# Three passes for the second expert of the first 448-column chunk, weights split in another order, and one row load moved, in a fused attention and expert kernel

## The chip, the cores and the metric

The kernel runs on one core of a Trainium2 chip. The metric is the device time of one execution in microseconds. The profile shows one execution; its times count from the start of the span.

## The reference

The first half is attention with a sketched kernel: q and k (4 batches, 4 heads, 1088 tokens, 32 wide) are each multiplied by two small matrices S1 and S2 (8 x 32), and the outer product of the two results is a feature of 64 numbers. The second half puts the heads side by side (4352 tokens, 128 wide) and runs four experts on every token, weighted by normalized probabilities.

```python
q_p, k_p = phi(q), phi(k)               # outer products of S1 x and S2 x, 64 features
kv = np.einsum('bhsf,bhsd->bhfd', k_p, v)
z = np.sum(k_p, axis=2)
x = (q_p @ kv) / (q_p @ z + 1e-6)       # per head; then heads side by side: (4352, 128)
p = domain_probs / (domain_probs.sum(-1, keepdims=True) + 1e-09)
for e in range(4):                      # w1[e]: 128 x 1024, w2[e]: 1024 x 128
    h = np.maximum(x @ w1[e], 0.0)
    out += p[:, e:e + 1] * (h @ w2[e])
```

All data is float32.

## The kernel before, in words

**Chunks and steps.** The tokens are the columns of all expert products. They are cut into chunks of 128, 448, 512, seven times 448, and 128 columns (`CHUNKS`, counted m = 0, 1, 2 and on). For each chunk the four experts follow each other, and for each expert the 1024 hidden rows are taken as eight blocks of 128, two blocks (a pair) to a step. So a chunk has `NQ` = 16 steps; step i is chunk i // 16, expert (i % 16) // 4, pair i % 4. A step has two half steps, j = 0 and 1, one block each. A half step is written (i.j) here: (20.0) is the first half of chunk 1's second expert (expert 1), (24.0) the first half of its third.

**Two kinds of product.** A plain product multiplies float32 operands directly. A product in three passes splits each operand into a high and a low part of a narrower type (`fp32r` in the profile) and a third, mixed part, and adds three products: for the first layer `xa`·`wa` (L1105), `xb`·`wb` (L1106) and `xd`·`wd` (L1154). Between the second and the third pass ScalarE scales the sum in PSUM in place (L1107, `h<-h`). The third pass of a half step is issued by `third()`, which is called in the next half step, after that one's first two passes. Then ScalarE makes the hidden tile: for blocks whose second product is in three passes (`THREE`, six of eight) the high part `ha` (L1157), from which VectorE makes `hb` (L1131) and, for two blocks at once, `hd` (L1134); for the others a plain relu, `hid` (L1162). The second layer's products are issued some half steps later by a list of due times (`to_due`, `DEAL`, `behind`; L1203 where the expert is plain, L1222 otherwise). VectorE adds their two sums into `ev` (L1254) after ScalarE copied one (L1225 or, for plain experts, L1251), and GpSimd multiplies by the gate and adds to the total (L1261, L1263).

**Which product is of which kind before.** Chunk 0 and the last chunk are plain throughout. In chunk 1 the first two experts are plain (`whole`: L1092 for the first layer with `hid` at L1094, L1203 for the second). All else is in three passes.

**Split weights.** `weight_parts(e)` makes `wa` on ScalarE and `wb`, `wd` on VectorE, 512 columns at a time, over four steps. `second_weight_parts(e)` makes `vab` on ScalarE twice (768 columns) and `vab`, `vb`, `vd` on VectorE, over two steps. `token_parts(m)` makes `xa` on ScalarE and `xb`, `xd` on VectorE for a chunk. All go through `split` (L882) and `join` (L885). The table `to_part` says after which step each is called; what is called at the end of a step stands on each engine's queue behind that step's own work.

**Attention beside the experts.** The tokens of chunk m must exist before the chunk starts. Attention is cut into units (`UNITS`); unit 1 of batch 0 is chunk 0, unit 2 (448 rows) chunk 1, and unit 3 (512 rows) chunk 2. Unit 2's stages on VectorE run during chunk 0; they end in a transposition `y` (L694) and copies into the tile `ring` on ScalarE and GpSimd (L706). Unit 3 is transposed (`qturn`), projected on TensorE (L243, `qT,sx`), copied by ScalarE (`qs`, L755), stored to DRAM (`qd`) and read back broadcast (`qp`, `qb`), multiplied on VectorE (L776), multiplied with the keys' sums on TensorE (`kvx`), divided, transposed to `y`, stored (`xd`) and loaded into `ring`. Batch 1's keys follow: transposition (`kT`, L383), projection (L426, `sk,kT`), `fs` and `vx` copies on ScalarE (L429, L392, L397), products on VectorE (L442). These pieces stand in one list, `plan`, each with a cost and, for some, a number of half steps that must lie between it and an earlier piece. `work()`, called once in every half step, adds a credit by the room that is left until the next chunk (`rate`, `rooms`, `EARLY`) and runs pieces while the credit lasts.

**Queues.** Nearly all DMAs are issued by SP, in program order. The rows of q for units 2 and 3 of batch 0 are one load (`load_rows(q, 0, "qn", slice(P, S))`, 960 columns) ahead of all expert weights; then follow `w1` of expert 0 (L141), the probabilities, `w2` of expert 0 (L154), and `w1`, `w2` of experts 1 to 3.

Of the kernel before, what the change touches and what calls it, by code (L numbers as in the profile page):

```python
# [24 lines left out]
def kernel(  # L25
# [26 lines left out]
    P = 128  # L52
# [45 lines left out]
    def load_rows(src, b, name, part=slice(0, S)):  # L98

        d = kn if name == "kn" else qn  # L100
        if b not in d:
            d[b] = lpool.tile([P, S], F32, tag=name, name=name)
        c, n = part.start, part.stop - part.start
        base = src.offset + b * H * S * D
        if name == "qn" and b == B - 1:
            for c, n, t in ((0, (G - 4) * D, 0), ((G - 4) * D, 4 * D, S - P)):
                nc.sync.dma_start(d[b][:, c : c + n], bass.AP(src.tensor, base + t * D, [[S * D, H], [n, 32], [1, n]]))
        else:
            nc.sync.dma_start(d[b][:, part], bass.AP(src.tensor, base + c, [[G * D, P], [1, n]]))
# [70 lines left out]

    ends = cpool.tile([P, 2, E], F32, name="ends")
    e_sum = cpool.tile([P, 2, 3], F32, name="e_sum")
    load_rows(q, 0, "qn", slice(P, S))
    load_w1(0)
    for p0, n, g0, m, t in ((0, 96, 0, G, 0), (96, 32, 0, G - 4, 3 * S), (96, 32, G - 4, 4, B * S - P)):
        nc.sync.dma_start(
# [9 lines left out]
    for e in range(1, E):  # L196
        load_w1(e)
        load_w2(e, 0)
        load_w2(e, 1)
    sk = cpool.tile([P, P], F32, name="sk")  # L200
    sp = apool.tile([32, 3, 2, 32], F32, tag="qf", name="sp")
    sr = cpool.tile([P, 3, 2, P], F32, tag="sr", name="sr")
# [592 lines left out]
    def add(cost, run, name, after=None):  # L795

        plan.append((cost, run, name, after))

    def lay_plan():

        of_first = queries(0, P, UNITS[0][1])
        costs = [0.62] * 9 + [0.05] * 4 + [0.4, 0.55, 0.6, 0.1, 0.1]
        for at, cost in enumerate(costs):
            add(cost, lambda: next(of_first, None), f"first{at}", ("first8", 5) if at == 12 else ("first12", 2) if at == 13 else None)
        covers.append((len(plan), P + UNITS[0][1]))
        add(vector_us(later[0][2]), lambda: unit_turn(0), "qturn")
        add(0.1, lambda: unit_project(0), "visit", ("qturn", 7))
        add(0, lambda: None, "wait", ("start", 2 * NQ + 2))
        keys = {}
        for b in range(1, B):  # L810
            now_on, plan[:] = list(plan), []
            key_pieces(b)
            keys[b], plan[:] = list(plan), now_on
        for w, (b, c, n, u) in enumerate(later):
            if b == 0:
                plan.extend(keys[1][:3])
            else:
                at = {(1, 0): (1, 3, 13), (1, 1): (2, 0, 3), (1, 2): (2, 3, 5), (2, 0): (2, 5, 13)}
                at.update({(2, 1): (3, 0, 3), (2, 2): (3, 3, 9), (3, 0): (3, 9, 13)})
                if (b, u) in at:  # L820
                    k, z0, z1 = at[b, u]
                    plan.extend(keys[k][z0:z1])
                if u == 0:
                    key_end(b)
            more = w + 1 < len(later)
            if more:
                add(vector_us(later[w + 1][2]), lambda w=w: unit_turn(w + 1), "qturn")
            for p in range(2):
                add(vector_us(n), lambda w=w, p=p: unit_product(w, p), "product", ("visit", LAND if w else LAND + 3))

            def visit(w=w, more=more):
                if more:
                    unit_project(w + 1)
                unit_visit(w)

            add(0.1, visit, "visit", ("product", 3 if w < 4 else 2))
            add(0.4, lambda w=w: inverse.__setitem__(w, attend_inverse(*products[w])), "inverse", ("visit", 1))
            add(vector_us(n), lambda w=w: over.__setitem__(w, attend_scale(*products[w], inverse.pop(w))), "scale")
            add(vector_us(n), lambda w=w: unit_out(w), "out")
            covers.append((len(plan), S * b + c + n))  # L840
# [196 lines left out]
    def whole(m, e):  # L1037
        return m == 1 and e < E // 2

    begun_hp, made_hp = {}, {}  # L1040

    def half_columns(i, hp, c):
# [11 lines left out]
    def first(i, work, between=None):  # L1054

        m, kq = steps[i]
        n, (e, f) = CHUNKS[m], divmod(kq, NP)
        if plain(m):
            third()
            lower()  # L1060
            hd = hidden()
            hid[i] = [hd[:, n * j : n * j + n] for j in range(2)]
            if i in begun_hp:
                hp = begun_hp.pop(i)
                half_columns(i, hp, HP)
            elif i in made_hp:
                hp = made_hp.pop(i)
            else:
                hp = psum(ps_h, "h")
                for j in range(2):  # L1070
                    both(
                        hp[:, n * j : n * j + n],
                        w1_of[e][:, P * (2 * f + j) : P * (2 * f + j + 1)],
                        (x_last if m else x_first)[:, :],
                        start=True,
                        stop=True,
                    )
            if m and kq % 2:
                nc.vector.tensor_scalar(
                    out=hd[:, 0 : 2 * n], in0=hp[:, 0 : 2 * n], scalar1=0.0, scalar2=None, op0=ALU.max  # L1080
                )
            else:
                nc.scalar.activation(hd[:, 0 : 2 * n], hp[:, 0 : 2 * n], ACTF.Relu)
            work()
            work()
            return
        hid[i] = []
        if whole(m, e):
            ((x, _, _),) = placed(START[m], n)
            for j in range(2):  # L1090
                hp = psum(ps_h, "h")[:, 0:n]
                nc.tensor.matmul(hp, w1_of[e][:, P * (2 * f + j) : P * (2 * f + j + 1)], x, start=True, stop=True)  # L1092
                u = hidden()[:, 0:n]
                nc.scalar.activation(u, hp, ACTF.Relu)  # L1094
                hid[i].append(u)
                work()
                if j == 0:
                    between(0)
            return
        xa, xb, xd_ = (x[:, 0:n] for x in xparts[m])  # L1100
        for j in range(2):
            k = 2 * f + j
            g = psum(ps_h, "h")[:, 0:n]
            w = slice(P * k, P * (k + 1))
            nc.tensor.matmul(g, wa[:, e, w], xa, start=True, stop=False)  # L1105
            nc.tensor.matmul(g, wb[:, e, w], xb, start=False, stop=True)  # L1106
            nc.scalar.activation(g, g, ACTF.Copy, scale=1.0 + R12)  # L1107
            third()
            hid[i].append(None)
            begun.append((i, j, k, g, wd[:, e, w], xd_))  # L1110

            if any(d[0] <= 2 * i + j and d[5] and d[5] + str(2 * (steps[d[3]][1] % NP) + d[4]) == last_of[1] for d in due):
                between(j)
                lower()
                work()
            else:
                lower()
                work()
                if j == 0:
                    between(0)  # L1120
# [28 lines left out]
    def third():  # L1149

        while begun:
            i, j, k, g, w, x = begun.pop(0)
            n = g.shape[-1]
            nc.tensor.matmul(g, w, x, start=False, stop=True, skip_group_check=True)  # L1154
            if in_three(k):
                (ha, hb, hc), both_of = three_tiles(k, n)
                nc.scalar.activation(ha, g, ACTF.Relu, scale=NEAR)  # L1157
                to_lower.append((g, ha.bitcast(F32), hb, both_of))
                hid[i][j] = ha, hb, hc
            else:  # L1160
                hid[i][j] = hidden()[:, 0:n]
                nc.scalar.activation(hid[i][j], g, ACTF.Relu)  # L1162
# [152 lines left out]
        begun_hp[i] = psum(ps_h, "h")  # L1315
        half_columns(i, begun_hp[i], 0)
    to_part = {}
    for e, at, then in zip((2, 3, 0, 1), (8, 15, 15, 18), (18, 20, 26, 32)):
        for at, parts_of in ((at, weight_parts(e)), (then, second_weight_parts(e))):
            for step in range(at, at + 4):  # L1320
                to_part.setdefault(step, []).append(parts_of)
    for m in range(1, NC - 1):
        at, tokens = NQ * m - 4 if m > 1 else NQ + 4, token_parts(m)
        for step in (at, at + 1):
            to_part.setdefault(step, []).append(tokens)
    ending = iter(())
# [42 lines left out]
    for i in range(len(steps) + LA):  # L1369
        if i < len(steps):  # L1370
# [2 lines left out]
            rate = max(  # L1373
                [0]
                + [
                    (needed[c] - spent[0]) / max(sum(rooms[2 * i : 2 * NQ * c - (EARLY if c > 1 else 2)]), 0.3)
                    for c in range(m + 1, NC)
                    if 2 * NQ * c - (EARLY if c > 1 else 2) > 2 * i
                ]
            )  # L1380

# [68 lines left out]
```

## Time and profile before

| what | value |
|---|---|
| times of the kernel before | 456.1, 456.46 and 496.8 us, median 456.46 |
| the profiled execution's own time | 456.12 us |
| its span | 454.3 us |
| granted TensorE clock in the span | 1.00 |
| busy: TensorE, VectorE, ScalarE, GpSimd | 447.6, 359.7, 329.3, 119.0 us |
| HBM read, written | 32.68 MB, 5.21 MB |
| chunk 0's experts on TensorE | about 13.4 to 30.1 us |
| chunk 1, experts 0 and 1 | about 30.1 to 56.4 us |
| chunk 1, experts 2 and 3 | about 56.4 to 79.4 us |

Rows of the profile name an engine, a source line, an operation, the tile written and the tiles read. PE is TensorE's products, PEld its weight loads, DVE VectorE, ACT ScalarE, POOL GpSimd, SPq the issuing of DMAs by SP. A plain float32 product is recorded as two rows (x2). The recorded length of a row is not the distance to the next one: rows of an engine overlap in the record, so the pace is read from the starts. A bracket at the end of a row is idle time of the engine just before it and what ended it. The chain of waits is the work that ended last, followed back from the end.

### The profile page before, as it was taken

What the parts mean: (1) busy time and instruction counts of PE and PEld (TensorE: products, weight loads), DVE (VectorE), ACT (ScalarE), POOL (GpSimd) and SP (SyncE); (2) the same over time, 40 slices, a digit from 0 to 9 for tenths busy, and PEclk for the clock granted to TensorE, in tenths of its full rate; (3) what the DMA queues carried; (4) which work ended last, traced back from release to release, by engine and by line L of the source; (5) the groups of instructions that cost most, each with busy time, mean ns of one, the idle gap of its engine ahead of it and who ended that gap; (6) DMA issues with size and microseconds to landing.
All of it is one profiled execution on the core that took longest, in us unless ns stands there. A gap on an engine that the chain in (4) does not pass through costs nothing.

```text
span 454.3 us, 8639 instructions
## 1 busy us (share of the span) xinstructions
PE 447.6 (99%) x3005; PEld 366.1 (81%) x3005; DVE 359.7 (79%) x600; ACT 329.3 (72%) x695; POOL 119.0 (26%) x206
## 2 busy tenths in 40 slices
PE   9999999999999999999999999999999999999997
PEld 6765587777778888888988888888888888888886
DVE  6867669988888797889877998787779787887753
ACT  4366588866877695788786867787778788877731
POOL 6462122410232123212221232124223212322320
PEclk9999999999999999999999999999999999999999
DMA  7884252024313353052423511320320121027401
GB/s 213 281 189 119 67 169 78 24 45 109 119 51 75 82 111 57 20 138 72 122 64 47 143 25 28 94 75 21 87 57 24 37 45 41 21 41 218 147 2 27
DMA packets 53716, 38.45 MB, mean 85 GB/s; under 512 B 27113, under 2 KB 49961, under 8 KB 53673
## 3 DMA queue, kind: packets, MB, share of 16 engines
q1 hardware_dynamic: 53272, 37.85, 32.1%
q8 instruction: 23, 0.38, 0.3%
q14 instruction: 21, 0.16, 0.1%
q0 software_dynamic: 384, 0.06, 0.1%
q10 hardware_dynamic: 16, 0.00, 0.0%
HBM read 32.68 MB, written 5.21 MB: 83 GB/s over the span
## 4 chain that ended last, share of the span: by engine, by line
PE 92%; DMA 2%; SPq 1%; DVE 1%; ACT 1%; issue 1%; ACTq 0%
PE o L1222 39%; PE h L1154 12%; PE h L1105 12%; PE h L1106 12%; PE h L243 7%; PE h L1092 3%; PE o L1203 3%; PE o L243 2%; PE h L426 1%; DMA w_sb<-in_moe_w_dram 1%; DMA vn<-in_v_dram 1%; SPq L154 1%; ACT ring L706 0%; SPq L115 0%; DVE wb L885 0%
## 5 line engine op out<-in xcount | busy, mean ns | idle before, releaser
L1107 ACT ACTIVATE h<-h 128x448 f32<-128x448 f32 (+1 forms) x272 | 146.9, 540 | 76.6 <-PE h L1106 71.0
L1131 DVE SCALAR_TENSOR_TENSOR hb<-h,ha 128x448 fp32r<-128x448 f32 (+1 forms) x204 | 125.9, 624 | 55.7 <-ACT ha L1157 54.3
L1105 PE MATMUL h<-xa,wa 128*128 128x448 f32 (+1 forms) x272 | 124.5, 458 | 0.0
L1134 DVE SCALAR_TENSOR_TENSOR hd<-ha,hb 128x896 fp32r<-128x896 f32 (+1 forms) x102 | 117.9, 1155 | 8.2
L1157 ACT ACTIVATE ha<-h 128x448 fp32r<-128x448 f32 (+1 forms) x204 | 111.6, 547 | 0.0
L1154 PE MATMUL h<-xd,wd 128*128 128x448 f32 (+1 forms) x272 | 100.8, 371 | 0.5 <-ACT h L1107 0.5
L1106 PE MATMUL h<-xb,wb 128*128 128x448 f32 (+1 forms) x272 | 100.2, 368 | 0.0
L1261 POOL TENSOR_TENSOR ev<-ev,gate 128x256 f32<-128x256 f32 (+1 forms) x54 | 40.9, 757 | 224.6 <-DVE ev L1254 206.8
L1222 PE MATMUL o<-ha,vab 128*128 128x448 f32 (+1 forms) x204 | 76.9, 377 | 0.0
L1105 PEld LDWEIGHTS h<-xa,wa 128*128 128x128 f32 x272 | 51.2, 188 | 17.1 <-issue 13.0
L1106 PEld LDWEIGHTS h<-xb,wb 128*128 128x128 f32 x272 | 51.2, 188 | 17.0 <-issue 13.1
L1222 PE MATMUL o<-hid,w_sb 128*128 128x448 f32 (+1 forms) x136 | 63.1, 545 | 0.1
L1222 PE MATMUL o<-hd,vd 128*128 128x448 f32 (+1 forms) x204 | 58.5, 368 | 0.0
L1154 PEld LDWEIGHTS h<-xd,wd 128*128 128x128 f32 x272 | 51.0, 187 | 8.9 <-ACT h L1107 2.7
L1222 PE MATMUL o<-hb,vb 128*128 128x448 f32 (+1 forms) x136 | 50.0, 369 | 0.0
L1263 POOL TENSOR_TENSOR total<-total,ev 128x256 f32<-128x256 f32 (+1 forms) x54 | 44.7, 827 | 4.2
L1222 PEld LDWEIGHTS o<-ha,vab 128*128 128x128 f32 x204 | 38.3, 188 | 4.5 <-issue 0.3
L1222 PEld LDWEIGHTS o<-hd,vd 128*128 128x128 f32 x204 | 38.3, 188 | 3.4
L1162 ACT ACTIVATE hid<-h 128x448 f32<-128x448 f32 (+1 forms) x68 | 37.8, 555 | 0.1
L1261 POOL TENSOR_TENSOR total<-ev,gate 128x256 f32<-128x256 f32 (+1 forms) x18 | 12.5, 714 | 76.2 <-issue 58.0
L1222 PEld LDWEIGHTS o<-hid,w_sb 128*128 128x128 f32 x136 | 25.5, 188 | 2.7 <-DVE ev L1254 0.5
L1222 PEld LDWEIGHTS o<-hb,vb 128*128 128x128 f32 x136 | 25.6, 188 | 1.9
(140 smaller groups left out, 468.6 us busy)
## 6 DMA issues: line engine op xcount, KB each, us to landing
gate<-gates SPq DMA_DIRECT2D x24, 224.0 KB
kn<-in_k_dram SPq DMA_DIRECT2D x4, 544.0 KB
vn<-in_v_dram SPq DMA_DIRECT2D x16, 128.0 KB
w_sb<-in_moe_w_dram SPq DMA_DIRECT2D x4, 512.0 KB
w_last<-in_moe_w_dram SPq DMA_DIRECT2D x4, 512.0 KB
qp<-qd SPq DMA_DIRECT2D x6, 224.0 KB
qb<-qd SPq DMA_DIRECT2D x6, 224.0 KB
out_dram<-ob SPq DMA_DIRECT2D x24, 56.0 KB
```

The source lines that it names most:

```text
L243: nc.tensor.matmul(out(s), weights(s), moving(s), **flags)
L1105: nc.tensor.matmul(g, wa[:, e, w], xa, start=True, stop=False)
L1106: nc.tensor.matmul(g, wb[:, e, w], xb, start=False, stop=True)
L1107: nc.scalar.activation(g, g, ACTF.Copy, scale=1.0 + R12)
L1131: nc.vector.scalar_tensor_tensor(out=hb, in0=g, scalar=0.0, in1=high, op0=ALU.max, op1=ALU.subtract)
L1134: nc.vector.scalar_tensor_tensor(out=d2, in0=a2.bitcast(F32), scalar=R12, in1=b2.bitcast(F32), op0=ALU.mult, op1=ALU.subtract)
L1154: nc.tensor.matmul(g, w, x, start=False, stop=True, skip_group_check=True)
L1157: nc.scalar.activation(ha, g, ACTF.Relu, scale=NEAR)
L1162: nc.scalar.activation(hid[i][j], g, ACTF.Relu)
L1222: nc.tensor.matmul(acc[m, e][o][:, 0:n], w, h, start=first_one, stop=last)
L1261: nc.gpsimd.tensor_tensor(out=to[:, x], in0=ev[:, x], in1=g[:, x], op=ALU.mult)
L1263: nc.gpsimd.tensor_tensor(out=total[m][:, x], in0=total[m][:, x], in1=ev[:, x], op=ALU.add)
```

## The change

- `three_first`: in chunk 1, expert 1's first product is now made in three passes, like that of experts 2 and 3. Its second product stays plain, so its hidden tile is a plain relu from `third()`.
- Split weights are made in the order of experts 1, 2, 3, 0, the first layer's from steps 12, 16, 20, 24 on (before: experts 2, 3, 0, 1 from steps 8, 15, 15, 18), the second layer's of experts 1, 2, 3, 0 from steps 32, 20, 24, 28 on (before, for experts 2, 3, 0, 1: 18, 20, 26, 32).
- Chunk 1's token parts are made after steps 17 and 18 instead of 20 and 21.
- Unit 3's rows of q (512 columns) become a load of their own, behind the weights of all experts; unit 2's 448 stay where both were.
- In the plan, unit 2's last pieces and unit 3's transposition, projection and product get other distances, and the time by which unit 2 must be done is set earlier (13 half steps ahead instead of 2).

```diff
-    load_rows(q, 0, "qn", slice(P, S))
+    load_rows(q, 0, "qn", slice(P, P + UNITS[0][1]))
     load_w1(0)
...
         load_w2(e, 0)
         load_w2(e, 1)
+    load_rows(q, 0, "qn", slice(P + UNITS[0][1], S))
...
+        distances = {12: ("first8", 5), 13: ("first12", 2), 16: ("first15", 2), 17: ("first16", 1)}
         for at, cost in enumerate(costs):
-            add(cost, lambda: next(of_first, None), f"first{at}", ("first8", 5) if at == 12 else ("first12", 2) if at == 13 else None)
+            add(cost, lambda: next(of_first, None), f"first{at}", distances.get(at))
...
-        add(vector_us(later[0][2]), lambda: unit_turn(0), "qturn")
-        add(0.1, lambda: unit_project(0), "visit", ("qturn", 7))
+        add(vector_us(later[0][2]), lambda: unit_turn(0), "qturn", ("start", 2 * NQ - 2))
+        add(0.1, lambda: unit_project(0), "visit", ("qturn", 6))
...
-                add(vector_us(n), lambda w=w, p=p: unit_product(w, p), "product", ("visit", LAND if w else LAND + 3))
+                add(vector_us(n), lambda w=w, p=p: unit_product(w, p), "product", ("visit", LAND if w else LAND + 1))
...
+    def three_first(m, e):
+        return not plain(m) and not (m == 1 and e == 0)
...
-        if whole(m, e):
+        if not three_first(m, e):
             ((x, _, _),) = placed(START[m], n)
...
-            if in_three(k):
+            if in_three(k) and not whole(steps[i][0], steps[i][1] // NP):
...
-    for e, at, then in zip((2, 3, 0, 1), (8, 15, 15, 18), (18, 20, 26, 32)):
+    for e, at, then in zip((1, 2, 3, 0), (12, 16, 20, 24), (32, 20, 24, 28)):
...
-        at, tokens = NQ * m - 4 if m > 1 else NQ + 4, token_parts(m)
+        at, tokens = NQ * m - 4 if m > 1 else NQ + 1, token_parts(m)
...
-                    (needed[c] - spent[0]) / max(sum(rooms[2 * i : 2 * NQ * c - (EARLY if c > 1 else 2)]), 0.3)
+                    (needed[c] - spent[0]) / max(sum(rooms[2 * i : 2 * NQ * c - (EARLY if c > 1 else 13)]), 0.3)
                     for c in range(m + 1, NC)
-                    if 2 * NQ * c - (EARLY if c > 1 else 2) > 2 * i
+                    if 2 * NQ * c - (EARLY if c > 1 else 13) > 2 * i
```

## The prediction

> **What bounds the kernel now.** The page comes first.
>
> ```profile
> span 454.3 us, 8639 instructions
> PE 447.6 (99%) x3005; PEld 366.1 (81%) x3005; DVE 359.7 (79%) x600; ACT 329.3 (72%) x695; POOL 119.0 (26%) x206
> ...
> PEclk9999999999999999999999999999999999999999
> ```
>
> TensorE is busy to the end, the granted clock full. The waits, asked for the whole run, tell what is left to remove:
>
> ```profile
> PE o L243 <- ACT hid L1083: 0.9, 1, 0.9
> ...
> PE h L243 <- DMA w_sb<-in_moe_w_dram: 0.7, 1, 0.7
> PE h L1154 <- ACT h L1107: 0.5, 1, 0.5
> ```
>
> Three waits of any size, 2.1 us: two in chunk 0 (at 17.14 and 29.48 us), one at 70.44. So the change is worth what it takes from TensorE's list, less the new waits. The chain of waits, 54 to 59 us, prices both kinds of product:
>
> ```profile
> 54.70 0.75 PE o L1203 x2
> 55.45 0.75 PE h L1092 x2
> 56.20 0.75 PE o L1203 x2
> 57.36 0.75 PE o L1203 x2
> 58.72 0.75 PE o L1203 x2
> ```
>
> A plain float32 product of 448 columns takes 0.75. From 57.36 to 58.72 lie one of these and three passes: 1.36 - 0.75 = 0.61 for the three. That is a gain of 0.14 per half step, with a new dependence: the third pass waits for ScalarE's copy of the first two (L1107). The timeline of TensorE and ScalarE shows what it costs when ScalarE is late:
>
> ```profile
> 68.10 0.55 ACT L1107 ACTIVATE h<-h 128x448 f32<-128x448 f32 x1
> ...
> 68.56 0.54 ACT L1157 ACTIVATE ha<-h 128x448 fp32r<-128x448 f32 x1
> 68.99 0.22 ACT L429 COPY fs<-h 128x64 f32<-128x64 f32 x1
> 69.08 0.87 ACT L882 ACTIVATE vab<-w_sb 128x768 fp32r<-128x768 f32 x1
> ...
> 69.82 0.56 ACT L1107 ACTIVATE h<-h 128x448 f32<-128x448 f32 x1
> ...
> 70.44 0.47 PE L1154 MATMUL h<-xd,wd 128*128 128x448 f32 x1 [0.45 <-ACT h L1107]
> ```
>
> One weight copy (vab) between two L1107 copies puts the second at 69.82, and the third pass, due at 69.82, runs at 70.44: 0.62 lost. Starts here are ScalarE's real pace: 0.44 after a 448 copy, 0.74 after vab; wa and xa 0.52. Elsewhere a copy starts 0.47 after the start of its second pass (56.99 to 57.46), and the third pass can start 0.60 after the copy. The windows of experts 2 and 3 of chunk 1 give the room there:
>
> ```profile
> 56.44:67.80 11.36, 11.36 (x58) 9.21 (x57) 6.89 (x10) 9.19 (x20) 3.35 (x4) 1.00 0.55 156
> 67.80:79.39 11.59, 11.14 (x52) 8.88 (x51) 11.02 (x19) 10.18 (x23) 3.06 (x4) 1.00 0.30 89
> ```
>
> Columns: length, busy time of PE, PEld, DVE, ACT, POOL, then clock and DMA. The second window is full on VectorE (11.02 of 11.59).
>
> **The change, part by part.** Durations are of the profiled execution: 456.12 us, its span 454.3 and 1.82 around it. It stands between the two lower runs (456.1 and the median 456.46), so its sum is taken as the median's. Steps are numbered 16 x chunk + 4 x expert + pair, halves .0 and .1.
>
> *Passes.* Expert 1 has eight half steps: 8 x (0.75 - 0.61) = -1.1.
>
> *Order on TensorE.* The third unit's projection (4 products, L243) moves from between two ring products to beside chunk 0's last output products. Both are half-width, so two changes of width go. One costs 0.95 - 0.75 = 0.2 (the chain's first product after a change against the others), less what is overlapped: -0.3 together.
>
> *Chunk 0.* Before, two copies to wb and one to wd lay among the third stage of unit 2 on VectorE. Only the wb at 25.35 held up y (25.95, then 0.70); the others hid behind the wait for TensorE's products at 22 to 23.7. So y ends 0.6 sooner, 26.05. The ring copies on ScalarE wait for the hidden tile at 26.02, so they start at 26.4, not 26.68. But wa of expert 1 now stands right behind them: +0.55 ahead of the hidden tile that started at 29.04. Net 0.3 later, and TensorE's product at 29.48 is what waits: +0.3.
>
> *Loads.* Rows of unit 3 (256 KB, one DMA more) leave their place ahead of the first weights and go behind the last. Expert 1's first weights, for which TensorE waits at 17.14, were issued at 12.39, when SP had worked through its list; from 9.4 to 12.4 the DMA engines were only 0.52 busy, so fewer bytes ahead bring them no sooner: 0 (bounds: 0 and -0.7, the whole wait; the share nearest to it says 0). Behind the weights the new issue delays gate stores and batch 1's loads by some 0.4 (a row load takes SP 0.35 to 0.43). VectorE already waits 1.2 at 33.16 for k rows; behind that stand the token parts xb, xd of chunk 1, ready near 38.7 by adding up VectorE's list and wanted at 42.7: 4 us of cover; a load later than that costs microsecond for microsecond. Transposing unit 3 now follows expert 1's wb and wd, about 31 instead of 27.14; batch 1's q load waits for it, 31.7 instead of 30.64, and the stores of qd stand behind it on SP. In the trace these were issued at 33.2 and landed at 39 behind other loads; issued 2.2 later they land at much the same time. The products from them ended at 60.87 (y) and the ring was first read at 71.78: 0.
>
> *Three passes in expert 1.* ScalarE gets eight L1107 copies, and vab of expert 2 and wa of expert 3 now stand between them. The stack before (21.0): relu 0.44, vab 0.74, wa 0.52, and the copy before it 0.44 = 2.14. Copy to third pass: 0.47 + 2.14 + 0.60 = 3.21 after the second pass of (20.1); due after two half steps, 2.72, and 0.20 = 2.92. Lost: +0.29. The backlog meets vab again at (22.0): +0.2. Plain products lost nothing to such stacks, their relu had two half steps of time.
>
> *Weight copies in steps 24 to 29.* (25.0): ha, vab, wa, the same 3.21 against 2.92: +0.3. Then the copy of (25.1) follows ha and the expert's ev copy, 0.44 + 0.51 + 0.43 behind the late one, while TensorE is only 0.61 further: its keys' products (L426, 0.9), which lay ahead of that third pass before, now lie behind it. 0.60 + 1.38 after 0.6: lost +0.8. (29.0): copy, ha, vx, vab, xa: 0.44 + 0.44 + 0.25 + 0.74 + 0.52 = 2.39; 0.47 + 2.39 + 0.60 = 3.46 against two short half steps, 1.22 + 1.02 + 0.20 = 2.44: +1.0, with the lag carried in +1.2. Gone: the 0.62 above and 0.15 at 72.90, since vab and xa leave those places: -0.8.
>
> *VectorE* takes 4.9 us more in steps 24 to 31: vab, vb, vd of expert 3, 2 x (0.42 + 0.68) = 2.2; wb and wd of expert 0, 2 x (0.69 + 0.65) = 2.7. 17.9 + 4.9 = 22.8 in a window of 22.95 that grows by ScalarE's 2.3. hb and hd have about two half steps of leave: 0, bounds 0 and +1.6 (below).
>
> Sum: -1.1 - 0.3 + 0.3 + 0.5 + 2.3 - 0.8 = **+0.9**, so 456.12 + 0.9 = **457.0 us**. From chunk 2 on the same work moves by a half step; no stack of that kind shows there.
>
> ScalarE's prices decide this. [...]
>
> **Rivals.**
>
> 1. *ScalarE keeps ahead.* The stacks are absorbed because vab and wa start when their sources are idle and copies come early. For: of many stacks before, one cost 0.62. Against: (29.0) has five instructions in a row. Without the 2.8, and with the old 0.8 gone: 456.12 - 1.1 - 0.3 + 0.3 - 0.8 = 454.2; half of it 455.6.
>
> 2. *VectorE becomes the bound of steps 24 to 32, slower.* In order, from the first hb 3 us into the window, it has 22.8 to do, and hd took 1.54 and 1.56 beside GpSimd at 61.65 and 78.46 instead of 1.09; six of these add 2.7. 3 + 22.8 + 2.7 - 22.95 = 5.6 late, less the window's 2.3 and two half steps (1.7 at chunk 1's shortest): +1.6, so 458.6. It decides from where hb of (28.1) misses its product at (30.0). For: the second window is full already. The Trainium skill (SBUF — State Buffer, SBUF: two separate sides) says that the loser of the port shared by VectorE and GpSimd is blocked for the other's whole instruction; by that an hd would lose up to 0.73, the length of a GpSimd row; the trace agrees in part, with 0.45.
>
> 3. *ScalarE's instructions cost their recorded times* (0.54, 0.85, 0.62) in a stack, not their pace. The stacks then cost 1.2, 1.8 and 1.7, 1.9 more: 459.0. Against: rows start 0.44 apart. [...]
>
> 4. *Split weights or token parts of expert 1 come late*, so that it doesn't run as meant: (20.0) waits. With k rows 4 us later than now the cost starts; 2 us beyond, 459.
>
> **How the numbers follow.** Forecast 457.0, its own range 456.0 to 458.0, chance 0.55; rival 1 with less (454.2 to 456.0) 0.23; rival 2 (458.0 to 459.5) 0.14; rival 3 0.03; rival 4 0.03; else 0.02. The range 454.8 to 458.8 leaves out half of rival 1's lower part, the top of the others. 2%, 9.1 us, is about what a measurement of this kernel can tell from no change; nothing above reaches it: faster 0.01, slower 0.03 (a stalled start, much later loads), within 0.96.
>
> **What would show it.** Right: products of the second expert 1.36 apart, not 1.50; TensorE's third passes waiting for the copy at three places, near 47, 60 and 72 us, together above 2 us; none where 70.44 was, in the middle of expert 2. Product for chunk 0 at 29.7 instead of 29.48; the weights' wait at 17.14 unchanged. Wrong: these waits under 1 us (rival 1); VectorE without a gap from 58 to 80 with TensorE waiting for hb (rival 2); a wait before the first three-pass product of expert 1 (rival 4).

## The result and the profile after

| | before | changed |
|---|---|---|
| time, median (us) | 456.41 | 458.24 (457.99 to 458.57) |
| profiled execution (us) | 456.12 | 458.49 |
| its span (us) | 454.3 | 456.7 |

The ratio is 1.0041, 95% interval 1.0027 to 1.0055: 1.8 us slower, far inside 2%. The forecast was 457.0, the range 454.8 to 458.8. The two profiled executions lie 2.4 apart; that difference is taken apart below. One run of before, 496.8, lies far above the other five and is left out of the ratio; without it the median of before is 456.37. Lines from L200 on stand one to five numbers higher than before (L1107 is now L1112, L1131 is L1136).

The page, engines and clock:

```profile
span 456.7 us, 8654 instructions
PE 447.6 (98%) x3013; PEld 367.2 (80%) x3013; DVE 357.8 (78%) x600; ACT 332.1 (73%) x703; POOL 120.8 (26%) x206
```

TensorE's eight additional rows are there (three instead of two in each half step of expert 1), and its busy time is what it was; VectorE's is even lower. So the loss is in waits. TensorE's waits over the whole run (engine, line, what was waited for, total us, times, longest):

```profile
PE o L244 <- ACT hid L1088: 1.2, 1, 1.2
PE h L1159 <- ACT h L1112: 1.2, 2, 0.7
PE o L1227 <- DVE hb L1136: 0.9, 2, 0.6
...
PE h L244 <- DVE kT L384: 0.5, 1, 0.5
PE o L1227 <- DVE ev L1259: 0.4, 1, 0.4
PE h L244 <- DMA w_sb<-in_moe_w_dram: 0.4, 1, 0.4
```

The chunk 0 wait grew from 0.9 to 1.2, the copies (L1112) hold the third pass twice instead of once, and two lines are new among the experts: second-layer products that wait for VectorE, for `hb` and for `ev`. (The line with `kT`, also new, is one wait at 6.09 us, at the start, where executions differ.) The chain of waits says that VectorE is the bound (start, us, what). Before, it ran mostly through TensorE's products here:

```profile
58.38 0.55 ACT ha L1162
58.95 0.62 DVE hb L1136
59.57 0.62 DVE y L695
...
63.36 1.89 DVE vd L887 x2
...
83.31 0.55 DVE hb L1136
83.90 0.87 PE o L1227 x3
```

From 58.95 to 83.9 every piece is VectorE's or is called issue, and the timeline has VectorE rows in those pieces too. The window of steps 28 to 32 (columns as in the prediction's windows) agrees:

```profile
67.80:80.00 12.20, 10.97 (x50) 8.45 (x49) 11.96 (x20) 10.36 (x23) 2.00 (x3) 1.00 0.29 89
```

VectorE is busy 11.96 of 12.20, TensorE only 10.97.

To see where the loss arises, the start of the first layer's second pass (L1106, now L1111; in expert 1 before, of the plain product) is compared half step by half step. A column is the delay against the kernel before, each from one profiled execution. Executions differ by about 1 us at the start, so steps within one column are what is read. (The five kernels of the columns are alike up to (16.0), and stand at +0.10 to +0.69 there.) The experiments (exp.) are told below.

| half step | before, at us | changed | exp. 1: split at 16 | exp. 5: 1 and copies | exp. 7: 1 and joins | exp. 2: 1 and second layers |
|---|---|---|---|---|---|---|
| (16.0) | 30.07 | +0.26 | +0.10 | +0.47 | +0.69 | +0.18 |
| (19.0) | 39.72 | -0.09 | -0.25 | +0.12 | +0.34 | -0.17 |
| (24.0) | 56.99 | -0.88 | -1.04 | -0.65 | -0.44 | -0.95 |
| (25.0) | 59.51 | -0.68 | -0.84 | -0.45 | -0.24 | -0.75 |
| (29.1) | 72.57 | -0.06 | -1.04 | -0.18 | +0.37 | -0.40 |
| (30.0) | 74.58 | +0.67 | -0.23 | +0.65 | +1.10 | -0.32 |
| (33.0) | 82.01 | +2.84 | +1.17 | +2.06 | +3.28 | -0.29 |
| (35.0) | 88.64 | +2.85 | +1.17 | +2.06 | +3.28 | -0.32 |
| (156.0) | 423.13 | +2.44 | +0.98 | +1.99 | +2.84 | +0.19 |
| (25.0) to (35.0) | | **3.53** | **2.01** | **2.51** | **3.52** | **0.43** |

The changed kernel is 0.88 ahead when expert 2 of chunk 1 begins, at (24.0). Expert 1's last third pass still stands behind that point; with it the lead is 0.68, at (25.0). It then loses 3.53 in ten steps, and 0.4 of that have come back by (156.0). (In between the delay falls for a half step or a few where a piece of attention has moved to the other side of the point, to +0.80 at (40.0) for example, and rises again.)

### The profile page after: what moved, and what is told of

It is laid out like the page before. It is cut to its first block, busy times and chain, and to the rows that moved or that the text cites. A ratio compares the mean times of both kernels' runs of the same rounds, so it can differ in the third digit from the quotient of the medians.

```text
span 456.7 us, 8654 instructions
## 1 busy us (share of the span) xinstructions
PE 447.6 (98%) x3013; PEld 367.2 (80%) x3013; DVE 357.8 (78%) x600; ACT 332.1 (73%) x703; POOL 120.8 (26%) x206
## 4 chain that ended last, share of the span: by engine, by line
PE 88%; DVE 5%; DMA 2%; SPq 1%; ACT 1%; issue 1%; ACTq 0%; DVEq 0%
PE o L1227 38%; PE h L1110 12%; PE h L1159 12%; PE h L1111 12%; PE h L244 8%; PE o L244 3%; PE o L1208 2%; PE h L1097 1%; DVE hb L1136 1%; DMA w_sb<-in_moe_w_dram 1%; DMA vn<-in_v_dram 1%; DVE hd L1139 1%; PE h L427 1%; DVE vd L887 1%; SPq L154 1%
## 5 line engine op out<-in xcount | busy, mean ns | idle before, releaser
L1112 ACT ACTIVATE h<-h 128x448 f32<-128x448 f32 (+1 forms) x280 | 151.3, 540 | 82.6 <-PE h L1111 76.7
L1136 DVE SCALAR_TENSOR_TENSOR hb<-h,ha 128x448 fp32r<-128x448 f32 (+1 forms) x204 | 125.9, 625 | 56.8 <-ACT ha L1162 55.6
L1110 PE MATMUL h<-xa,wa 128*128 128x448 f32 (+1 forms) x280 | 130.0, 464 | 0.1
L1139 DVE SCALAR_TENSOR_TENSOR hd<-ha,hb 128x896 fp32r<-128x896 f32 (+1 forms) x102 | 115.7, 1134 | 8.2
L1159 PE MATMUL h<-xd,wd 128*128 128x448 f32 (+1 forms) x280 | 103.8, 371 | 1.3 <-ACT h L1112 1.2
L1111 PE MATMUL h<-xb,wb 128*128 128x448 f32 (+1 forms) x280 | 103.1, 368 | 0.0
L1266 POOL TENSOR_TENSOR ev<-ev,gate 128x256 f32<-128x256 f32 (+1 forms) x54 | 41.9, 776 | 221.9 <-DVE ev L1259 203.4
L1227 PE MATMUL o<-ha,vab 128*128 128x448 f32 (+1 forms) x204 | 76.5, 375 | 0.0
L1110 PEld LDWEIGHTS h<-xa,wa 128*128 128x128 f32 x280 | 52.7, 188 | 18.9 <-issue 13.9
L1111 PEld LDWEIGHTS h<-xb,wb 128*128 128x128 f32 x280 | 52.7, 188 | 18.3 <-issue 14.4
L1227 PE MATMUL o<-hid,w_sb 128*128 128x448 f32 (+1 forms) x136 | 63.2, 546 | 0.4 <-DVE ev L1259 0.4
L1159 PEld LDWEIGHTS h<-xd,wd 128*128 128x128 f32 x280 | 52.5, 187 | 10.1 <-ACT h L1112 3.9
L1227 PE MATMUL o<-hd,vd 128*128 128x448 f32 (+1 forms) x204 | 58.8, 369 | 0.0
L1227 PE MATMUL o<-hb,vb 128*128 128x448 f32 (+1 forms) x136 | 50.4, 372 | 0.9 <-DVE hb L1136 0.9
L1167 ACT ACTIVATE hid<-h 128x448 f32<-128x448 f32 (+1 forms) x76 | 42.2, 556 | 0.1
L1227 PEld LDWEIGHTS o<-ha,vab 128*128 128x128 f32 x204 | 38.3, 188 | 4.4 <-issue 0.3
L1227 PEld LDWEIGHTS o<-hd,vd 128*128 128x128 f32 x204 | 38.0, 188 | 3.3
L1227 PEld LDWEIGHTS o<-hb,vb 128*128 128x128 f32 x136 | 25.6, 188 | 4.1 <-DVE hb L1136 1.9
L1227 PEld LDWEIGHTS o<-hid,w_sb 128*128 128x128 f32 x136 | 25.3, 188 | 3.5 <-DVE ev L1259 1.3
```

The source lines that it names most:

```text
L1136: nc.vector.scalar_tensor_tensor(out=hb, in0=g, scalar=0.0, in1=high, op0=ALU.max, op1=ALU.subtract)
L1139: nc.vector.scalar_tensor_tensor(out=d2, in0=a2.bitcast(F32), scalar=R12, in1=b2.bitcast(F32), op0=ALU.mult, op1=ALU.subtract)
L1227: nc.tensor.matmul(acc[m, e][o][:, 0:n], w, h, start=first_one, stop=last)
L1266: nc.gpsimd.tensor_tensor(out=to[:, x], in0=ev[:, x], in1=g[:, x], op=ALU.mult)
```

## The experiments

All are edits of the changed kernel except where it is said. Theory A: the loss is the splitting of expert 0's and 3's weights in steps 24 to 31, on ScalarE and VectorE. B: it comes from the row load and the pieces of attention. C: it comes from the three passes of expert 1.

**1. Expert 0's first layer split at step 16 instead of 24.**

```diff
-    for e, at, then in zip((1, 2, 3, 0), (12, 16, 20, 24), (32, 20, 24, 28)):
+    for e, at, then in zip((1, 2, 3, 0), (12, 16, 20, 16), (32, 20, 24, 28)):
```

> Expert 0's first-layer split goes from steps 24 to 27 to steps 16 to 19, all else as changed. Theory A (the loss is weight-splitting work that was pulled into steps 24 to 31: ScalarE's stacks between two in-place copies, and VectorE's queue of 4.9 us more): wa leaves the stack at (25.0), which cost 0.3 there and 0.7 behind it, and VectorE has 2.7 us less, so it is no longer the bound of steps 30 to 33, which cost 2.2: about 455.8 to 456.6 us. Theory B (the moved row load and what waits for it): no change, 458.2. Theory C (the half-step shift of the attention pieces, above all the keys' projection behind the third pass of (25.1)): 457.5 to 458.2.

Measured: 457.24 us, ratio 1.0021 (1.0011 to 1.0032). One number in the table of weights takes back half of the loss, so A holds in kind. It is less than A expected: the second layers' splits of experts 3 and 0 were still where they were, and (25.0) to (35.0) still loses 2.01.

**2. The second layers of experts 3 and 0 two steps earlier as well.**

```diff
-    for e, at, then in zip((1, 2, 3, 0), (12, 16, 20, 24), (32, 20, 24, 28)):
+    for e, at, then in zip((1, 2, 3, 0), (12, 16, 20, 16), (32, 20, 22, 26)):
```

> As the run before, and the second-layer splits of experts 3 and 0 go from steps 24 and 28 to 22 and 26, so that vab and xa no longer stand together at (29.0). Theory A: the stack at (29.0) falls from 1.2 lost to about 0.3, but one with vab and the v copy appears at (28.0), about 0.7; VectorE has 1.1 us less to do from step 24 on: 455.3 to 456.2. Theory B: 458.2. Theory C: 457.5 to 458.2.

Measured: 455.68 us, ratio 0.9988 (0.998 to 0.9996), now ahead of the kernel before. TensorE no longer waits for `hb` or `ev`; of the lines above, the copies' is left, with the same total:

```profile
PE h L1159 <- ACT h L1112: 1.2, 2, 0.7
```

These are other waits, though: 0.49 at 70.01, where a new stack with `vab` and the v copy was expected to cost about 0.7, and 0.68 at 122.91, in chunk 2. Loss from (25.0) to (35.0): 0.43. Both numbers are places in the table; no work was taken out. With experiment 1 it settles that the splits' place is the cause: 1.5 of the 3.53 hang on expert 0's first layer, 1.6 on the second layers.

**3. The rows of units 2 and 3 loaded together, ahead of the weights.**

```diff
-    load_rows(q, 0, "qn", slice(P, P + UNITS[0][1]))
+    load_rows(q, 0, "qn", slice(P, S))
...
-    load_rows(q, 0, "qn", slice(P + UNITS[0][1], S))
```

> Unit 3's rows are loaded with unit 2's again, ahead of the weights; all else as changed. Theory A: within 0.4 us of 458.2; the wait for expert 1's weights at about 17 us goes from 0.35 back to 0.73 (up to 0.4 more), and nothing later moves. Theory B: back by most of the 1.8 us that the change lost: 456.5 to 457. Theory C: 458.2.

Measured: 459.14 us, ratio 1.0064 (1.0041 to 1.0087). The loss stays. The median is 0.9 above the changed kernel's, more than the 0.4 that A allowed, but the intervals overlap; the wait for expert 1's weights, which was to grow, is absent from this run's trace. B falls as far as the load goes.

**4. Expert 1 of chunk 1 plain again, all else changed.**

```diff
-        return not plain(m) and not (m == 1 and e == 0)
+        return not plain(m) and not (m == 1 and e < 2)
```

> Expert 1's first product is plain again; weight order, token parts, plan and loads stay as changed. Theory A: 8 x 0.14 = 1.1 us come back to TensorE's list and the copies' waits in expert 1 (0.5) go: +0.6 at the start of step 24, and the later losses stay, a little smaller as VectorE starts step 24 with more done: 458.4 to 459. Theory B and C: +0.6: 458.8. If the three passes themselves cost the time, it falls to 456.4 to 457.

Measured: 459.48 us, ratio 1.0068 (1.0056 to 1.008). Without the passes the kernel is 1.2 us slower still, so C falls. It is also more than the 0.2 to 0.8 that A expected. In the trace 0.58 of it stands from (19.0) to (25.0), where the passes are: the changed kernel gains 0.59 there, this one 0.01. From (25.0) to (35.0) it loses 3.51, as the changed kernel does. Another 0.6 comes up at (46.0), far from them: ScalarE's copy to `xa` for the next chunk, ahead of a copy in place (L1112), waits for a load there, and a third pass waits behind it.

```profile
124.83 0.58 ACT L884 ACTIVATE xa<-ring 128x448 fp32r<-128x448 f32 x1 [0.64 <-DMA ring<-xd]
```

**5. Which engine: spare copies on ScalarE.** Experiment 1, with two copies of 512 columns to a spare buffer behind steps 24 and 26, where `wa` of expert 0 stood.

```diff
+        for _ in range(2):
+            split(spare[:, :], w1_of[0][:, 0 : F // 2], 4096.0)
+            yield
...
+    for step in (24, 26):
+        to_part.setdefault(step, []).append(copies)
```

> Expert 0's first-layer split at steps 16 to 19 as in the first of these runs, and two ScalarE copies of the same size (512 columns into a buffer that is not read) put where its wa stood in the changed kernel, after steps 24 and 26. So ScalarE has its old stacks and VectorE is 2.7 us lighter. If ScalarE's stacks cost the time of steps 24 to 33, it is back to 458.2; if VectorE's backlog does, it stays near 457.2 (the run without the copies), plus the 0.3 to 0.7 of the stack at (25.0): about 457.5, and no product waits for hb. If neither: 457.2.

Measured: 457.64 us, ratio 1.0033 (1.0016 to 1.0049). The copies add 0.50 to the loss of experiment 1, nearly all of it from (25.0) to (29.1) (0.27 lost there, where experiment 1 gains 0.20). From (30.0) on they add nothing. Against the expectation products do wait for `hb` (0.9 in all), as they do in experiment 1 (0.8).

**6. Which engine: spare joins on VectorE.** Experiment 1, with four joins behind steps 24 to 27, where `wb` and `wd` stood.

```diff
+        for _ in range(4):
+            join(spare[:, :], w1_of[0][:, 0 : F // 2], -4096.0, wa[:, 0, 0 : F // 2].bitcast(F32), ALU.add)
+            yield
```

> The counterpart: expert 0's split at 16 to 19, and four VectorE joins of the same size and operands (into a buffer that is not read) after steps 24 to 27, where wb and wd stood. ScalarE stays lighter, VectorE has its old load. If VectorE's backlog costs the time: near 458.2, less the 0.3 to 0.7 of ScalarE's stack: about 457.6 to 458, with the waits for hb and ev back at steps 31 to 33. If ScalarE's stacks cost it: 457.2.

Measured: 458.33 us, ratio 1.0047 (1.0031 to 1.0064), the changed kernel's time again. But the trace spoils the conclusion. The joins read the raw weights, whose buffer expert 0's `vab` takes over, and ScalarE's copy to `vab` waited for one of them:

```profile
72.47 0.84 ACT L884 ACTIVATE vab<-w_sb 128x768 fp32r<-128x768 f32 x1 [0.77 <-DVE spare L887]
```

The third pass behind it waited 1.6. That wait isn't in the changed kernel, so the run doesn't tell how much is VectorE's queue alone.

**7. The same joins, from finished parts.** They read `wa` and `wb`, which nothing overwrites.

```diff
-            join(spare[:, :], w1_of[0][:, 0 : F // 2], -4096.0, wa[:, 0, 0 : F // 2].bitcast(F32), ALU.add)
+            join(spare[:, :], wa[:, 0, 0 : F // 2].bitcast(F32), -R12, wb[:, 0, 0 : F // 2].bitcast(F32), ALU.subtract)
```

> The kernel with expert 0's first-layer weights split at step 16, and four spare joins of 512 columns put on VectorE after steps 24 to 27, which read the finished wa and wb of expert 0 and so hold no buffer that ScalarE's later vab wants. (With the spare joins that read the raw weights, ScalarE's vab waited 0.77 us for one of them.) Theory that VectorE's queue alone is the second way of the loss: the same four joins on VectorE without that wait on ScalarE still cost 4 x 0.6 = 2.4 us of its time, less the gaps of 1.1 us it had there, and beside GpSimd more: 457.9 to 458.4, the loss between the half steps (30.0) and (33.0) near 2.2 us as in the changed kernel, 1.4 without the joins, and TensorE waiting for hb and ev. Rival, that the joins cost only by the wait they put on ScalarE: 457.1 to 457.5, the loss from (30.0) to (33.0) near 1.4 and from (25.0) to (30.0) near 0.6.

Measured: 458.72 us, ratio 1.0051 (1.0033 to 1.0068), above the 457.9 to 458.4 expected; the loss between the half steps is as expected. (25.0) to (35.0) loses 3.52, the changed kernel's 3.53, and the parts are the same too: 0.61 and 0.62 up to (29.1), 0.73 and 0.73 to (30.0), 2.18 and 2.17 to (33.0). TensorE's waits match those of the changed kernel:

```profile
PE h L1171 <- ACT h L1124: 1.0, 2, 0.7
PE o L1239 <- DVE hb L1148: 0.9, 2, 0.6
PE o L1239 <- DVE ev L1271: 0.4, 1, 0.4
```

(L1171, L1124, L1239, L1148, L1271 are the changed kernel's L1159, L1112, L1227, L1136, L1259.) So VectorE's joins alone are enough for the whole of what expert 0's first layer cost. ScalarE's copies cost 0.5 where VectorE has room (experiment 5), and nothing on top where it has none: the two don't add.

**8. Splits moved ahead wherever there was room.**

```diff
-    for e, at, then in zip((1, 2, 3, 0), (12, 16, 20, 24), (32, 20, 24, 28)):
+    for e, at, then in zip((1, 2, 0, 3), (13, 16, 16, 18), (32, 18, 23, 21)):
```

> The changed kernel with all splits of the first layer in steps 13 to 21 (experts 1, 2, 0, 3 from 13, 16, 16, 18) and the second layer's of experts 2, 3, 0 from 18, 21, 23, so that no half step has wa and vab together and steps 25 to 31 have only xa. If weight-splitting work is the cause, both losses go: the 0.5 in expert 1 and nearly all of steps 24 to 33, and expert 0's hidden tile in chunk 0 no longer stands behind wa: 454.4 to 455.2 us, below the kernel before. If the plan or the loads cost the time: 456 or more.

Measured: 454.74 us, ratio 0.9966 (0.9954 to 0.9978). This is faster than both kernels: by the ratios 1.5 us ahead of before, 3.4 of the changed one. VectorE has gaps again where it had none, in which it waits for ScalarE's `ha` (in brackets):

```profile
64.38 0.62 DVE L1136 SCALAR_TENSOR_TENSOR hb<-h,ha 128x448 fp32r<-128x448 f32 x1 [1.67 <-ACT ha L1162]
...
67.86 0.62 DVE L1136 SCALAR_TENSOR_TENSOR hb<-h,ha 128x448 fp32r<-128x448 f32 x1 [0.86 <-ACT ha L1162]
```

**9. The kernel before, with only the passes and the table of experiment 8.** It keeps its own loads, plan and distances; chunk 1's token parts are made after 17 and 18, and `third()` has its new condition.

```diff
+    def three_first(m, e):
+        return not plain(m) and not (m == 1 and e == 0)
...
-    for e, at, then in zip((2, 3, 0, 1), (8, 15, 15, 18), (18, 20, 26, 32)):
+    for e, at, then in zip((1, 2, 0, 3), (13, 16, 16, 18), (32, 18, 23, 21)):
```

> The kernel before with the three passes of expert 1, chunk 1's token parts at 17 and 18 and the split times of the run before this one; its own loads and plan. If plan and loads do not matter: within 0.5 us of that run, 454.4 to 455.4. If the changed plan and the late row load bring something of their own: 0.5 to 1 us above it. If they cost something: below it.

Measured: 454.86 us, ratio 0.9971 (0.9959 to 0.9983), as experiment 8. The rest of the change, loads and plan, brings or costs nothing that shows in the time.

**10. Experiment 8 with expert 1 plain.** The edit of experiment 4 on that of 8.

> The fastest run so far (all splits of the first layer in steps 13 to 21) with expert 1's first product plain again: the price of the passes where no split stands among them. By the chain, 8 x 0.14 = 1.1 us more: 455.6 to 456.0. If the copies between the passes cost as much as the passes save, no difference: 454.7.

Measured: 455.23 us, ratio 0.9978 (0.9968 to 0.9988). The passes are worth some 0.5 here (0.0012 of 456), less than the 1.1 of the sum; the two intervals overlap. A part of what is missing is in the trace of experiment 8: splits do stand among expert 1's passes there, and one copy to `vab` puts off a third pass, a wait that the trace without the passes does not have.

```profile
42.63 0.84 ACT L884 ACTIVATE vab<-w_sb 128x768 fp32r<-128x768 f32 x1
...
43.96 0.47 PE L1159 MATMUL h<-xd,wd 128*128 128x448 f32 x1 [0.55 <-ACT h L1112]
```

From (19.0) to (25.0) the passes bring 0.33 in experiment 8, against 0.59 in the changed kernel.

**11. Experiment 8 with chunk 2's token parts a step later.**

```diff
-        at, tokens = NQ * m - 4 if m > 1 else NQ + 1, token_parts(m)
+        at, tokens = NQ * m - (3 if m == 2 else 4) if m > 1 else NQ + 1, token_parts(m)
```

> The fastest run so far with chunk 2's token parts one step later (29 and 30 instead of 28 and 29), so that xa no longer stands behind ha and the small v copy at (29.0), where the third pass waits 0.6. If that wait is what is left of ScalarE's stacks: 0.3 to 0.6 less, 454.1 to 454.4. If xb and xd then come too late for the chunk's first third pass: 0.3 or more above 454.7.

Measured: 455.13 us, ratio 0.997 (0.9959 to 0.9981). A miss: no gain. The wait of 0.6 that it aimed at isn't at (29.0): in experiment 8 it is the one at 43.96, in expert 1, and here it stands at 44.76 (0.56). The delay against before is -1.06 at (32.0) and -0.41 at (33.0), where experiment 8 has -1.51 and -1.54: chunk 2's first third pass comes late, at 80.21. The view puts its wait down to ScalarE's `hid`, which ends at 80.08; VectorE's `xd`, which the pass reads, is made from 79.38 to 80.06. So the expectation's other case, token parts that come too late, is the likely one.

**12. Experiment 8 with the rows of experiment 3.**

> The fastest run so far with unit 3's rows loaded together with unit 2's, ahead of the weights, as before. If the place of the rows is worth nothing: 454.7, within 0.3. If fewer bytes ahead of the first weights shorten the wait for expert 1's weights in most executions: 0.4 to 0.9 more, 455.1 to 455.6. If the late load holds up batch 1's loads: up to 0.4 less.

Measured: 454.83 us, ratio 0.9963 (0.995 to 0.9975), the same as experiment 8. The place of unit 3's rows is worth nothing that can be measured.

## Why the prediction came out as it did

The direction was right and the time lies in the stated range, 1.2 us above the forecast. But it lies outside the forecast's own range (456.0 to 458.0) and in the band of rival 2 (458.0 to 459.5), which had a chance of 0.14: the stated range holds it because it reaches over the rivals. The sum by its terms, against the changed column of the table (the pair of profiled executions lies 2.4 apart, the medians 1.8):

| term | forecast | measured, from where to where |
|---|---|---|
| chunk 0's product waits longer | +0.3 | +0.26 (the wait, 0.94 to 1.20) |
| order on TensorE | -0.3 | -0.35, (16.0) to (19.0) |
| passes of expert 1 with its two stacks | -1.1 + 0.5 | -0.59, (19.0) to (25.0) |
| stacks in steps 24 to 29, less the old ones | +2.3 - 0.8 | +1.35, (25.0) to (30.0) |
| VectorE | 0 | **+2.17**, (30.0) to (33.0) |
| chunk 2 and on | 0 | -0.40, (33.0) to (156.0) |
| sum | +0.9 | +2.44 |

*Chunk 0.* Right: the wait is 1.20 to 1.22 in every run with the changed kernel's splits in chunk 0, and 0.68 or 0.69 in those with the table of experiment 8. That the delay at (16.0) is +0.26 as well is chance, as executions differ there by more.

*Order on TensorE.* Right: -0.35 in every run with the changed plan, 0.00 in experiment 9, which keeps the old one.

*Passes.* Right in the trace and by experiment 4. Their products stand 1.36 apart with two longer distances, as the stacks foretold.

*ScalarE's stacks.* The sum fits, and the stack at (29.0) is in the timeline as it was worked out: four ScalarE rows between two copies, and a third pass that waits.

```profile
71.13 0.54 ACT L1162 ACTIVATE ha<-h 128x448 fp32r<-128x448 f32 x1
71.55 0.29 ACT L398 COPY vx<-vn 64x128 f32<-64x128 f32 x1
71.74 0.85 ACT L884 ACTIVATE vab<-w_sb 128x768 fp32r<-128x768 f32 x1
72.49 0.62 ACT L884 ACTIVATE xa<-ring 128x512 fp32r<-128x512 f32 x1
73.01 0.53 ACT L1112 ACTIVATE h<-h 128x448 f32<-128x448 f32 x1
73.59 0.47 PE L1159 MATMUL h<-xd,wd 128*128 128x448 f32 x1 [0.71 <-ACT h L1112]
```

It cost 0.71 instead of 1.2, and the third passes waited 1.2 in all at two places (0.44 at 61.97), where above 2 at three were expected. By the starts there are three: a third pass mostly starts 0.20 after the second pass ahead of it, and those at 47.16, 60.65 and 61.97 start 0.25, 0.26 and 0.61 later than that, where +0.29, +0.3 and +0.8 were expected. Taking the second layers away (experiment 2) leaves 0.08 from (29.1) to (30.0), against 0.73 to 0.83 in every kernel of the table that keeps them. The 0.62 lost up to (29.1), though, can't be given to ScalarE's copies alone: experiment 7 loses 0.61 there without those of expert 0. The total of this term fits partly by chance.

*VectorE, the step that failed.* The prediction wrote "hb and hd have about two half steps of leave: 0, bounds 0 and +1.6", and put its mechanism among the rivals, at 458.6. It came true together with the stacks. Two things that rival 2 counted and the sum did not used that leave up. VectorE enters the window late: its first `hb` there starts at 58.95. And it is slowed beside GpSimd, by joins this time, not by `hd`:

```profile
62.36 1.60 POOL L1268 TENSOR_TENSOR total<-total,ev 128x256 f32<-128x256 f32 x1
63.28 0.97 DVE L887 SCALAR_TENSOR_TENSOR vd<-vab 128x256 fp32r<-128x256 f32 x1
63.92 0.78 POOL L1266 TENSOR_TENSOR ev<-ev,gate 128x192 f32<-128x192 f32 x1
64.17 1.09 DVE L887 SCALAR_TENSOR_TENSOR vd<-vb,vab 128x512 fp32r<-128x512 f32 x1
64.79 0.92 POOL L1268 TENSOR_TENSOR total<-total,ev 128x192 f32<-128x192 f32 x1
65.18 1.08 DVE L887 SCALAR_TENSOR_TENSOR wd<-wa,wb 128x512 fp32r<-128x512 f32 x1
...
71.90 0.68 DVE L887 SCALAR_TENSOR_TENSOR wd<-wa,wb 128x512 fp32r<-128x512 f32 x1
```

The last row is the same join without GpSimd. By the starts, the three cost 0.55, 0.41 and 0.40 more than alone, and two at 78.09 and 79.23 cost 0.54 and 0.55: 2.45 in all, close to the 2.7 that rival 2 took. That the two figures are near is luck: rival 2 meant six `hd`, and every `hd` from 62 to 82 us took its 1.09. In the kernel before two `hd` had lost 0.92 in this stretch, so the change adds some 1.5. Rival 2's price was 1.6, and 2.2 was measured. That ScalarE's waits would lengthen VectorE's window and so relieve it was no protection: VectorE was without a gap all the same. Experiment 7 shows the price by VectorE's joins alone, and experiments 1 and 2 show it by moving the splits: with the splits some steps earlier all but 0.43 of the loss is gone.

*Loads.* Right: 0 (experiments 3, 9 and 12). The weights' wait at 17 us was 0.4 instead of 0.7; it went from none (experiment 3) to 2.1 (experiment 9) in other executions, so this says nothing.

*Chunk 2 and on.* The 0.4 that comes back there was not foreseen. It comes back between (46.1) and (64.0), where experiments 1, 2, 4, 8 and 10 gain 0.40 to 0.44 too, and experiment 9 gains nothing. So it goes with the loads and the plan that experiment 9 leaves as before; which piece it is isn't shown.

## What to carry to other kernels

When preparation is moved, its cost is set by the stage in which it lands: the same splits cost 3.1 us where VectorE was full, and next to nothing two to eight steps earlier. Where the sum shows an engine as full to within a per cent (22.8 of 22.95), don't leave the rest to slack in its consumers: add what it enters late and what it loses to another engine, and take that as the forecast. A spare load put in one engine's queue tells which queue decides, provided that it holds no buffer that another engine wants: the joins of experiment 6 held one, those of experiment 7 didn't.

## What the runs showed of the hardware that was not expected

- A join with two operands in SBUF beside a GpSimd row took 0.97 instead of 0.42 (256 columns), and 1.08 to 1.23 instead of 0.68 (512 columns); `hb`, which reads one operand from PSUM, was not slowed (two of them took 1.14 at 80.38, beside GpSimd). Where `hd` (1.09, not slowed) ran from 62.27, it was the GpSimd row at 62.36 that took 1.60, against 0.73 for the same shape at 117.82, with no such VectorE row beside it: the one that starts later pays. The Trainium skill (SBUF — State Buffer, SBUF: two separate sides) names this case, a VectorE operation with two SBUF inputs against a GpSimd operation that reads SBUF, and an exclusive lock for the whole instruction; the rows agree in which operations pay, and nearly in how much. When the five joins started, 0.68, 0.53, 0.53, 0.67 and 0.68 of the GpSimd row beside them were left, and they lost 0.55, 0.41, 0.40, 0.54 and 0.55: the rest of the other's row less some 0.13. The GpSimd row at 62.36 lost 0.87, where 1.00 of `hd` was left.
- Delays of ScalarE and VectorE in one stretch did not add here: with the joins alone the loss from (25.0) to (35.0) was 3.52, with the joins and the copies 3.53, though the copies alone added 0.50.
